# First GEMM by halves, w_in decoded in eight pieces, and zero matmuls ahead of the first scores

## The chip, the cores and the metric

One core of one Trainium2 chip. The metric is the device time of one execution in microseconds (us). Three runs of the kernel before took 536.71, 537.28 and 537.35 us; the median is 537.28.

## What is computed

The reference chains three parts, in float32 at the interface:

```python
attn_out = _attn_ref(q, k, v)              # (2, 8, 576, 64): heads 0-3 see a plain window of 32,
                                           # heads 4-7 a window dilated by 4
x = attn_out.transpose(0, 2, 1, 3).reshape(1152, 512)
h = x @ w_in                               # w_in is 512 x 1024, float64
e = np.exp(h - h.max(-1, keepdims=True))
solu = h * (e / (e.sum(-1, keepdims=True) + 1e-09))
ln = (solu - mu) / np.sqrt(var + 1e-06) * g_ln
x = ln @ w_out                             # w_out is 1024 x 512, float64
p = domain_probs / (domain_probs.sum(-1, keepdims=True) + 1e-09)
for e in range(4):                         # w1: 4 x 512 x 1024, w2: 4 x 1024 x 512
    out += p[:, e:e + 1] * (np.maximum(x @ w1[e], 0.0) @ w2[e])
```

## The kernel before, in words

Every matrix product of full precision is done as three products of float32r halves (high x high, high x low, low x high), so each operand is split into a high and a low part.

The work is cut into generators whose steps (one `yield` each) stand one by one in the text `ORDER` (line 25 on). The scheduler is manual: a loop over `ORDER` (from line 614) runs the next step of the generator named, and each engine executes its own instructions in just that order. Each engine waits for the instruction at the head of its queue; SyncE (SP) issues the loads in the order of the `l..` entries. A "+" behind a name sends the step's variable instruction to another engine: `pick()` then gives GpSimd and not VectorE, and `copy()` VectorE and not ScalarE.

- `UP.t.b`, `UD.t.b` (`att_U`, line 238): an attention unit, of the plain or the dilated heads, third t of sequence b; 12 units of 12 steps. Step 1: mask matmuls (line 245) and scores (line 254) on TensorE; 2: maximum (line 262) and 3: subtraction (line 264) on VectorE; 4: exponential on ScalarE (line 267); 5: sum, 6: reciprocal on VectorE; 7: product into a probability tile `pd` (line 273, `pick`); 8: six transposes (line 279); 9: copy to `pt` (`copy`); 10: product with v (line 292); 11: high part to `xhi` (`copy`); 12: low part to `xlo` (line 231, VectorE).
- `VI.j` (`conv_in`, line 195): w_in row block j, decoded from float64 by `convert` (line 169): two ScalarE steps (lines 173, 175), shift (line 177) and merge (line 179) on VectorE, addition (line 181, `pick`), high part (`copy`), low part (line 206, `pick`). Blocks 1, 2 and 3 are decoded 1024 columns at a time, block 0 in two halves (`VI.0`, `VI.4`). `VO.j.t` (`conv_out`) does the same for w_out in eight pieces of 512 columns; its low part is line 222 on VectorE.
- `H.t` (`moe_H`, line 315): 128 tokens of the first GEMM, 24 matmuls of 512 columns (line 321); the four row blocks of w_in are the outer loop and the two halves of the output columns the inner, and `HCUT` says how many row blocks make a step. Then maximum, exponential, product with sum (line 330) and scaling.
- `T.t` (`moe_T`): transposes of those 128 tokens (line 349), squares (line 351), high and low part. `X.c.dp` (`moe_X`): second GEMM (line 370), 384 tokens, half of the outputs; `XCUT` cuts it into steps, each for one or more of the four w_out blocks.
- `sc` (`scales`, line 580): small VectorE steps and one power on GpSimd for the normalisation. `WP`, `XQ`, `WV`: splits of w1, x and w2 for the expert part (line 402); `u`, `d` (`up`, line 483 in `product`; `down`, line 553): the two products of the experts, which then run in a plain loop to the end.

PSUM has two pools of two tiles: `psa` for scores, transposes and products with v, `psm` for H and X; a step that needs a third tile waits until the tile before the last has been read.

Ahead of `ORDER`, GpSimd builds the mask and VectorE clears the three probability tiles (lines 124, 125):

```python
for pd in pds:
    nc.vector.memset(pd, 0.0)
```

Of the kernel before, what the change touches and what calls it, by code (L numbers as in the profile page):

```python
# [28 lines left out]
UP.1.0 UP.0.0 lI.3 UP.0.0 UP.0.0 UD.2.0 VI.4+ UP.1.0 UP.2.0 lD.1 lO.0.0 lvp.2.0 VI.2 VI.1+ UP.1.0+ UD.1.0 UD.1.0 H.0 UD.1.0 UD.0.0 VI.2 UD.2.0 VI.2
UP.1.0 UD.0.0 VI.2+ UP.0.1 VI.1 VI.1 UP.1.0 UP.0.1 UD.0.0 VI.3 UP.0.1 UD.0.0 UD.0.0 VI.3 H.0 UD.2.0 UP.1.0 UD.2.0 VI.3 VI.3 UP.1.0 UP.2.0 UD.0.1 UP.0.1  # L30
lO.0.1 UP.1.0 UP.2.0 H.1 lP.1.1 VI.3+ UD.1.1 UD.0.1 VI.2 misc H.1 UP.2.0+ VI.3 VI.3+ UP.0.1 VO.0.1 UD.0.1 UD.0.1 VI.2 VO.0.1 UD.2.0 H.0 VO.0.0 H.0
UD.0.1 UD.1.1 UP.0.1 UD.1.1 VO.0.0 UD.2.0 endE UP.2.0 UP.0.1 UD.1.1 UD.2.0 UP.0.1 UD.0.1 H.0 UP.2.0 VO.0.1 VO.0.0 H.1 UP.2.0 H.0 VO.0.0 lvp.0.1 H.1
UP.0.1 lvd.2.1 H.0 UD.0.1+ VO.0.1 UP.2.0 UP.2.0 H.0+ H.1 UP.0.1 VO.0.0+ T.0 lvd.0.1 UP.0.1+ UP.0.1 VO.0.1+ UD.1.1 VO.0.0 T.0 VO.0.0 lO.1.0 T.0 H.2
UD.2.1 lO.1.1 T.0 UD.2.1 VO.1.0 UD.2.1 UD.0.1 H.1 H.1 UD.0.1 UD.2.1 H.2 VO.1.0 UD.2.1 VO.1.0 UD.0.1 H.1+ UD.1.1 T.1 UD.0.1 VO.1.0 UD.1.1+ VO.0.1 VO.1.1
T.1 H.2 H.3 UD.0.1 lvd.1.1 UP.2.1 T.1+ T.1 VO.1.0+ UD.1.1 H.2 VO.1.0 H.3 lO.2.0 UD.2.1 VO.0.1 UD.1.1 UP.2.1 lvp.1.1 H.2 UD.2.1+ VO.1.1 UP.2.1 VO.1.0
VO.2.0 VO.1.1 UD.1.1 VO.1.1 H.2+ H.3 VO.1.1+ VO.2.0 T.2 UD.1.1 T.2 VO.2.0 H.3 VO.2.0 UD.1.1 lO.2.1 UP.2.1 H.3 VO.1.1 H.4 T.2 VO.2.1 VO.1.1 VO.2.1 T.2
VO.2.1 H.3+ UP.2.1 UP.1.1 UP.2.1 UD.2.1 H.4 lvp.2.1 UP.1.1 VO.2.0+ VO.2.0 H.4 VO.2.1 lO.3.0 X.0.1 UP.1.1 UP.1.1 VO.2.1 UD.2.1 H.4 VO.2.0 VO.2.1 UP.2.1+
VO.2.1 VO.3.0 UP.1.1 VO.3.0 UP.2.1 UD.2.1 UP.1.1 UP.2.1 lO.3.1 UP.1.1+ VO.3.0 UD.2.1 VO.3.1 VO.3.0 X.0.0 UP.1.1 VO.3.1 VO.3.1 UD.2.1 VO.3.0 VO.3.0
VO.3.1 VO.3.1 H.4 UP.2.1 VO.3.1 VO.3.0 VO.3.1 X.0.1 UP.2.1 UP.1.1 UP.2.1 UP.1.1 endA UP.1.1+ X.0.1 X.0.0 T.3 X.0.0+ H.5 UP.1.1 T.3 T.4 H.5 T.4 H.5 H.6
H.5 T.3 H.5 H.7 H.5+ H.6 T.4 T.3 H.6 H.6 T.5 T.5 T.4 H.7 H.8 H.6 T.5 H.7 T.6 T.6 H.7 T.5 T.6+ X.1.0 X.1.0 H.8 H.8 T.6 H.7+ H.8 H.8+ T.8 T.7 X.1.1 T.7  # L40
T.8 endH X.1.0 T.7 lW.0 sc X.1.1 T.8 T.7 XQ.0 WP.0 T.8 X.1.1 WP.0+ WP.0 XQ.0 XQ.0 WP.0 WP.0+ XQ.0 X.2.0 WP.0 X.2.1 XQ.0 XQ.0 XQ.0 XQ.0 X.2.0 XQ.0 XQ.0+
WP.0 XQ.0 WP.0 XQ.0 WP.0+ lV.0 XQ.0 XQ.0 WP.0 WP.0 endX WP.0+ XQ.0 XQ.0 u.0 WP.0 WP.0 WP.0+ u.0 WP.0 u.0 WV.0 lW.1 X.2.1+ XQ.1 XQ.1 XQ.1 u.0 u.0 u.0
WV.0 u.0 u.0 WP.0 XQ.1 XQ.1 u.0 u.0 XQ.1 WP.0 XQ.1 u.0 u.0 WV.0 u.0 u.0 XQ.1 u.0 u.0 u.0 XQ.1 XQ.1 u.0 u.0 u.0 u.0 XQ.1 u.0 u.0 u.0 u.1 XQ.1 u.1 XQ.1
XQ.1 u.1 u.1 XQ.1 XQ.1 u.1 WP.1 WV.0 u.1 u.1+ u.1 u.1 WP.1 WP.1 WP.1 u.1 WP.1 u.1 u.1 u.1 u.1 u.1 WP.1 u.1 u.1 d.2 d.1 WP.1+ WP.1 u.1 d.2 lV.1 u.1 u.1
# [672 lines left out]
```

## Time and profile before

| | |
|---|---|
| runs, median (lowest to highest) | 537.28 us (536.71 to 537.35) |
| profiled execution | 536.57 us |
| its span | 534.8 us |
| TensorE busy | 520.2 us (97%), 3660 matmuls |
| VectorE busy | 349.6 us (65%) |
| ScalarE busy | 198.9 us (37%) |
| GpSimd busy | 166.8 us (31%) |
| granted TensorE clock | 1.00 |

The span runs from the first to the last instruction; all times inside it count from its start. "Busy" is the time in which an engine executes an instruction; the rest is waiting. A share over the whole span hides that stages differ: the first 30 us, the attention stage to some 94 us, the two GEMMs to some 155 us and the experts each have their own limit.

### The profile page before, as it was taken

To read this page: it belongs to the slowest core of one execution; us is meant where nothing else is said; L and a number is where in the kernel's file an instruction comes from. 1 tells how busy PE (TensorE), PEld (TensorE's weight loads), DVE (VectorE), ACT (ScalarE), POOL (GpSimd) and SP (SyncE) were. 2 spreads that over 40 slices of the span, in tenths; PEclk is the share of its full clock that TensorE was granted. 3 is DMA by queue.
4 is the path that set the end of the run, shared out by engine and by line. 5 is a ranking of instruction groups with operands and counts; after the bars stand their busy time and mean duration, and the time that the engine had idled before them with its cause. 6 is when DMAs were issued, how large, how long until landed. Compare 5 with 4: busy or idle time off the path is not lost.

```text
span 534.8 us, 8713 instructions
## 1 busy us (share of the span) xinstructions
PE 520.2 (97%) x3660; PEld 465.8 (87%) x3660; DVE 349.6 (65%) x472; ACT 198.9 (37%) x302; POOL 166.8 (31%) x121
## 2 busy tenths in 40 slices
...
GB/s 326 406 214 101 64 135 1 0 1 20 60 132 65 119 2 0 159 1 0 98 60 1 1 157 1 0 102 58 1 1 158 0 1 79 1 1 0 2 80 97
DMA packets 16856, 36.21 MB, mean 68 GB/s; under 512 B 3376, under 2 KB 3632, under 8 KB 16176
## 3 DMA queue, kind: packets, MB, share of 16 engines
...
q8 instruction: 29, 0.48, 0.4%
...
## 4 chain that ended last, share of the span: by engine, by line
PE 94%; DMA 2%; DVE 2%; ACT 1%; issue 0%; SPq 0%; DVEq 0%; ACTq 0%
PE pm L553 18%; PE pa L553 18%; PE pm L483 17%; PE pa L483 17%; PE pm L321 10%; PE pm L370 8%; PE pa L292 2%; PE pa L349 2%; DMA draw<-in_moe_w_in_dram 2%; PE pa L279 1%; DMA rw<-in_moe_w_dram 1%; PE pa L254 1%; ACT pt L159 0%; DVE sm L264 0%; PE pa L245 0%
## 5 line engine op out<-in xcount | busy, mean ns | idle before, releaser
L496 DVE SCALAR_TENSOR_TENSOR hl<-ct,hh 128x512 fp32r<-128x512 f32 (+1 forms) x64 | 61.5, 980 | 32.4 <-ACT hh L494 32.4
L494 ACT ACTIVATE hh<-ct 128x512 fp32r<-128x512 f32 (+1 forms) x64 | 42.2, 682 | 51.9 <-DVE ct L526 22.9
L553 PE MATMUL pm<-wh,hh 128*128 128x512 f32 (+1 forms) x148 | 56.9, 384 | 0.6 <-DVE xf L558 0.6
L483 PE MATMUL pa<-xoh,hl 128*128 128x256 f32 (+1 forms) x192 | 56.9, 296 | 0.0
L483 PE MATMUL pm<-xoh,hl 128*128 128x256 f32 (+1 forms) x192 | 56.8, 296 | 0.0
L483 PE MATMUL pm<-xol,hh 128*128 128x256 f32 (+1 forms) x192 | 56.8, 296 | 0.0
L483 PE MATMUL pa<-xol,hh 128*128 128x256 f32 (+1 forms) x192 | 56.8, 296 | 0.0
L553 PE MATMUL pm<-wl,hh 128*128 128x512 f32 (+1 forms) x148 | 56.8, 384 | 0.0
L483 PE MATMUL pm<-xoh,hh 128*128 128x256 f32 (+1 forms) x192 | 56.8, 296 | 0.0
L483 PE MATMUL pa<-xoh,hh 128*128 128x256 f32 (+1 forms) x192 | 56.8, 296 | 0.0
L553 PE MATMUL pm<-wh,hl 128*128 128x512 f32 (+1 forms) x148 | 56.7, 383 | 0.0
L553 PE MATMUL pa<-wl,hh 128*128 128x512 f32 x144 | 56.1, 390 | 0.0
L553 PE MATMUL pa<-wh,hh 128*128 128x512 f32 x144 | 56.1, 390 | 0.0
L553 PE MATMUL pa<-wh,hl 128*128 128x512 f32 x144 | 56.0, 389 | 0.0
L510 POOL TENSOR_TENSOR ct<-ct,ct 128x512 f32<-128x512 f32 (+1 forms) x15 | 22.4, 1492 | 78.7 <-ACT ct L508 52.6
L402 POOL TENSOR_TENSOR wl<-wl,wh 128x1024 fp32r<-128x1024 f32 x7 | 16.9, 2413 | 95.7 <-ACT wh L159 95.7
L558 DVE SCALAR_TENSOR_TENSOR xf<-pm,pr,xf 128x512 f32<-128x512 f32 (+1 forms) x33 | 24.1, 730 | 32.9 <-PE pm L553 32.9
L159 ACT CAST wh<-wl 128x1024 fp32r<-128x1024 f32 x16 | 16.8, 1053 | 71.0 <-PE pa L553 40.6
L558 DVE SCALAR_TENSOR_TENSOR xf<-pa,pr,xf 128x512 f32<-128x512 f32 x31 | 23.1, 746 | 29.4 <-PE pa L553 29.4
L483 PEld LDWEIGHTS pm<-xoh,hh 128*128 128x128 f32 x192 | 36.4, 190 | 0.3
L483 PEld LDWEIGHTS pm<-xol,hh 128*128 128x128 f32 x192 | 36.4, 190 | 0.3
L483 PEld LDWEIGHTS pa<-xol,hh 128*128 128x128 f32 x192 | 36.4, 190 | 0.3
...
## 6 DMA issues: line engine op xcount, KB each, us to landing
...
```

The source lines that it names most:

```text
L159: nc.scalar.copy(out, in_)
L292: nc.tensor.matmul(po[64 * row:64 * row + 64, 0, o:o + 96], lhsT=vv, rhs=pt[:, j, :, g, :], start=True, stop=True)
L321: nc.tensor.matmul(pm[:, n, :], lhsT=xx[:, kk, cols], rhs=ww["in", kk][:, 512 * n:512 * n + 512], start=(n_ == 0 and i < 2), stop=(n_ == K ...
L349: nc.tensor.transpose(pa[:, f // 4, (f % 4) * 128:(f % 4) * 128 + 128], e[:, f // 4, (f % 4) * 128:(f % 4) * 128 + 128], ident)
L370: nc.tensor.matmul(pm[:, dd, 0:CW], lhsT=w_, rhs=x_[:, f, :], start=(f == 0 and i == 0), stop=(f == KF - 1 and i == 2))
L402: pick().tensor_tensor(out=out, in0=a, in1=b, op=op)
L483: nc.tensor.matmul(ps[:, ff, 0:n], lhsT=a[:, kk, fc], rhs=b[:, kk, :], start=kk == 0 and m == 0, stop=kk == 1 and m == 2)
L494: nc.scalar.activation(out=hv, in_=src, func=AF.Relu)
L496: nc.vector.scalar_tensor_tensor(out=lv, in0=src, scalar=0.0, in1=hv.bitcast(F32), op0=ALU.max, op1=ALU.subtract)
L510: poolv().tensor_tensor(out=c12, in0=c21, in1=c22, op=ALU.add)
L553: nc.tensor.matmul(po[:, u, 0:dn], lhsT=h_[:, f, cols], rhs=w_, start=(f == 0 and i == 0), stop=(f == 3 and i == 2))
L558: nc.vector.scalar_tensor_tensor(out=acc[:, t, dc], in0=po[:, u, 0:dn], scalar=pr[:, t, e:e + 1], in1=acc[:, t, dc], op0=ALU.mult, op1=ALU ...
```

## The change

- `wz`, a tile of zeros, is cleared by VectorE, and `warm(8)` puts eight matmuls of zeros, 512 columns each, first on TensorE; `warm.4` in the order puts four more behind the scores of `UD.2.0`. Their PSUM tile belongs to `psm`; nothing reads it.
- The three probability tiles are cleared on GpSimd.
- w_in is loaded and decoded in eight pieces of 512 columns (`VI.0` to `VI.7`; j + 4 is the second half of block j), each with its own raw tile; the decoded words go through four buffers of 512 columns (`cvp`), which w_out shares, and w_out's raw words through two (`crp`).
- `moe_H` has the halves of the output columns as the outer loop and the row blocks as the inner; a half is finished before the other begins. `HCUT` and `XCUT` cut H and X finer.
- The order is another throughout, up to the expert loop.
- g_ln and the domain probabilities are laid out on the host so that each partition's values lie together in memory.
- `up` reads `hb[s]` inside `block`; that issues nothing.

```diff
-KORD = (0, 1, 2, 3)
-HCUT = (1, 1, 2, 2, 4, 2, 4, 4, 4)
-XCUT = (2, 2, 4)
+HCUT = (1, 1, 1, 1, 2, 2, 2, 4, 4)
+XCUT = (1, 1, 2)
...
+lP.0.0 UP.0.0 UP.0.0 UP.0.0 UP.0.0 UP.0.0 UP.0.0 UP.0.0 UP.0.0 lI.0 VI.0 VI.0 lD.0 UD.1.0 UP.0.0 VI.0 VI.0 UD.0.0 UD.1.0 UD.1.0 UD.1.0 VI.0+
+VI.0 VI.0+ UD.0.0 UD.0.0 UD.1.0 UD.1.0 lvp.0.0 UP.0.0 UP.0.0 UP.0.0 UD.0.0 lP.1.0 UP.1.0 UD.0.0 UD.1.0+ UD.0.0 UP.1.0 UP.1.0 UD.0.0+ lI.7 VI.7 UD.2.0
+VI.7 lI.2 lI.3 UD.2.0 VI.2 warm.4 UD.0.0 VI.2 lvd.0.0 lvp.1.0 UD.2.0 lD.1 lI.1 UP.2.0 UP.1.0 VI.7 VI.7 VI.2 UP.1.0 UP.1.0 UP.1.0+ lvd.1.0
...
+T.1 H.3 UP.1.1 H.4 VO.3.0 VO.2.0+ VO.0.0 VO.2.0 VO.3.0 UP.1.1+ H.4 H.4 H.4 UP.1.1 T.2 UP.1.1 H.3 H.3+ UP.2.1+ UP.2.1 VO.2.0 VO.3.0
+VO.3.0 VO.3.0 VO.3.0 H.4 UP.2.1 X.0.0 X.0.0 VO.3.0 H.4 H.4 lO.2.1 UP.1.1 VO.2.1 UP.2.1 UP.1.1+ UP.1.1 X.0.1 X.0.1 lO.3.1 VO.3.1 VO.3.1 VO.2.1
+VO.2.1 VO.2.1 VO.3.1 VO.2.1 VO.2.1 VO.2.1 X.0.0 H.4+ VO.3.1 VO.3.1 VO.3.1 VO.3.1 X.0.0 endA X.0.0 UP.2.1 UP.2.1 X.0.1 X.0.1 T.3 T.3 X.0.1+
+T.4 T.4 H.6 H.6 H.6 H.6 H.6 H.6 H.6 H.5 H.5 H.5 H.5 H.5 H.7 H.7 T.3 T.3 H.6+ H.5 H.5 H.5
+T.6 T.4 T.4 T.6 T.6 T.5 T.5 T.5+ H.7 T.5 H.7 H.7 H.7+ H.8 H.8 H.8 H.8 H.8 H.8+ X.1.0 X.1.0 X.1.0
+T.6 T.8 T.7 T.7 X.1.0 T.8 sc endH T.8 T.8 X.1.0 lW.0 T.7+ X.1.1 T.7 X.1.1 X.1.1 X.1.1 WP.0 XQ.0 X.1.1+ WP.0+
...
+    wz = const.tile([128, 512], BF16, name="wz")
+    nc.vector.memset(wz.bitcast(U32), 0)
+    wps = psm.tile([128, 2, 512], F32, name="pm", tag="pm")
+
+    def warm(n):
+        for i in range(n):
+            nc.tensor.matmul(wps[:, i % 2, :], lhsT=wz[:, 0:128], rhs=wz, start=True, stop=True)
+
+    warm(8)
...
-    cv = at.enter_context(tc.tile_pool(name="cv", bufs=1))
+    cvp = at.enter_context(tc.tile_pool(name="cvp", bufs=4))
+    crp = at.enter_context(tc.tile_pool(name="crp", bufs=2))
...
     for pd in pds:
-        nc.vector.memset(pd, 0.0)
+        nc.gpsimd.memset(pd, 0.0)
...
     def load_in(j):
         j, half = j % 4, j // 4
-        if half:
-            nc.sync.dma_start(out=dins[j][:, 1024:2048].bitcast(I64), in_=w_in[128 * j:128 * j + 128, 512:1024])
-            return
-        r = dins[j] = erp.tile([128, 2048], I32, name=f"draw{j}", tag=f"draw{j}")
-        n = 512 if j == 0 else 1024
-        nc.sync.dma_start(out=r[:, 0:2 * n].bitcast(I64), in_=w_in[128 * j:128 * j + 128, 0:n])
+        r = dins[j, half] = erp.tile([128, 1024], I32, name=f"draw{j}{half}", tag=f"draw{j}{half}")
+        nc.sync.dma_start(out=r.bitcast(I64), in_=w_in[128 * j:128 * j + 128, 512 * half:512 * half + 512])
...
-        sl = slice(512 * half, 512 * half + (512 if j == 0 else 1024))
+        sl = slice(512 * half, 512 * half + 512)
...
-        a = (erp.tile([128, 1024], F32, name="eva", tag="eva") if j % 2 else cva)[:, sl]
-        yield from convert(dins[j][:, 2 * sl.start:2 * sl.stop], a)
+        a = cvp.tile([128, 512], F32, name="cva", tag="cva")
+        yield from convert(dins[j, half], a)
...
     def moe_H(t):
         pm = psm.tile([128, 2, 512], F32, name="pm", tag="pm")
         cols = slice(128 * t, 128 * t + 128)
-        for n_, kk in enumerate(KORD):
-            seq = [(xhi, whi, n) for n in range(2)] + [(xhi, wlo, n) for n in range(2)] + [(xlo, whi, n) for n in range(2)]
-            for i, (xx, ww, n) in enumerate(seq):
-                nc.tensor.matmul(pm[:, n, :], lhsT=xx[:, kk, cols], rhs=ww["in", kk][:, 512 * n:512 * n + 512],
-                                 start=(n_ == 0 and i < 2), stop=(n_ == KD - 1 and i >= 4))
-            if n_ % HCUT[t] == HCUT[t] - 1:
-                yield
+        for n in range(2):
+            for kk in range(KD):
+                for i, (xx, ww) in enumerate(((xhi, whi), (xhi, wlo), (xlo, whi))):
+                    nc.tensor.matmul(pm[:, n, :], lhsT=xx[:, kk, cols], rhs=ww["in", kk][:, 512 * n:512 * n + 512],
+                                     start=(kk == 0 and i == 0), stop=(kk == KD - 1 and i == 2))
+                if (n * KD + kk) % HCUT[t] == HCUT[t] - 1:
+                    yield
...
     def load_misc():
-        nc.sync.dma_start(out=g_sb, in_=g_ln.rearrange("(f p) -> p f", p=128))
-        nc.sync.dma_start(out=pr_raw, in_=probs.rearrange("(t p) e -> p t e", p=128))
+        nc.sync.dma_start(out=g_sb, in_=g_ln)
+        nc.sync.dma_start(out=pr_raw, in_=probs.rearrange("p (t e) -> p t e", t=NTT))
...
+    d["moe_g_ln"] = d["moe_g_ln"].reshape(-1, 128).T
+    p = d["moe2_domain_probs"]
+    d["moe2_domain_probs"] = p.reshape(-1, 128, p.shape[1]).transpose(1, 0, 2).reshape(128, -1)
```

## Rows read from the trace of the kernel before

**Rows 1.** Windows: length, busy time (instructions) of PE, PEld, DVE, ACT, POOL, PEclk, DMA

```profile
10.00:15.00 5.00, 3.91 (x133) 2.26 (x123) 4.49 (x11) 3.10 (x6) 2.35 (x3) 1.00 1.02 425
...
22.93:85.54 62.61, 61.63 (x702) 50.08 (x701) 57.92 (x96) 50.53 (x79) 23.03 (x16) 1.00 0.39 135
...
138.40:531.00 392.60, 392.02 (x2312) 358.19 (x2313) 248.97 (x298) 114.17 (x174) 129.92 (x80) 1.00 0.14 47
```

**Rows 2.** Timeline of TensorE, first 30 us: start, duration, instruction, count, idle before

```profile
3.49 0.48 PE L245 MATMUL pa<-mask,identb 128*128 128x192 bf16 x2 [3.49 <-POOL mask L114]
5.68 0.97 PE L254 MATMUL pa<-qkP 64*32 64x64 f32 x48 [1.72 <-DMA qkP<-in_qkp_dram]
...
9.16 0.97 PE L254 MATMUL pa<-qkD 64*32 64x64 f32 x48 [2.08 <-DMA qkD<-in_qkd_dram]
...
16.10 1.54 PE L279 MATMUL pa<-ident,pd 128*128 128x128 f32 x6
...
19.04 1.35 PE L279 MATMUL pa<-ident,pd 128*128 128x128 f32 x6
...
23.64 0.82 PE L279 MATMUL pa<-ident,pd 128*128 128x128 f32 x6
```

**Rows 3.** Timeline of VectorE, first 45 us

```profile
3.68 2.87 DVE L125 MEMSET pd<- 128x960 f32 x3
6.47 0.36 DVE L177 TENSOR_SCALAR cva<-cva 128x512 uint32<-128x512 uint32 x1
...
10.17 0.56 DVE L262 TENSOR_REDUCE st<-pa 128x6 f32<-128x384 f32 x1 [1.56 <-PE pa L254]
...
14.31 0.68 DVE L177 TENSOR_SCALAR cva<-cva 128x512 uint32<-128x512 uint32 x1
...
43.15 1.22 DVE L330 SCALAR_TENSOR_TENSOR e<-e,pm 128x1024 f32<-128x1024 f32 x1
```

**Rows 4.** VectorE's groups, 0 to 95 us: count, busy, mean ns, idle before

```profile
L179 DVE SCALAR_TENSOR_TENSOR eva<-draw,eva 128x1024 uint32<-128x1024 uint32 x2 | 2.4, 1220 | 0.0
...
L181 DVE CUSTOM_DVE_ANT_0 cva<-cvr,cva 128x1024 uint16<-128x1024 uint16 x3 | 2.1, 686 | 0.0
...
L179 DVE SCALAR_TENSOR_TENSOR cva<-draw,cva 128x512 uint32<-128x512 uint32 x2 | 1.4, 684 | 0.0
```

**Rows 5.** Timeline of ScalarE, first 36 us

```profile
4.41 0.67 ACT L173 ACTIVATE draw<-draw 128x512 int32<-128x512 uint32 x1 [2.39 <-DMA draw<-in_moe_w_in_dram]
...
13.40 0.53 ACT L267 ACTIVATE sm<-sm 128x384 f32<-128x384 f32 x1 [0.40 <-DVE sm L264]
```

**Rows 6.** Timeline of GpSimd, first 36 us

```profile
0.73 0.20 POOL masks.py:197 MEMSET ident<- 128x128 f32 x1 [0.29 <-POOLq L700]
...
4.69 0.12 POOL L121 MEMSET mhalf<- 128x9 f32 x1
...
13.88 1.79 POOL L273 TENSOR_TENSOR pd<-sm,st 128x384 f32<-128x384 f32 x2
```

**Rows 7.** Timeline of SyncE's DMA queue

```profile
23.22 6.26 SPq L605 DMA_DIRECT2D pr_raw<-in_moe_domain_probs_dram  x1
31.35 2.31 SPq L142 DMA_DIRECT2D vp<-in_vpw_dram  x1
```

**Rows 8.** The chain that ended last: start, duration, what

```profile
84.19 4.36 PE pm L370 x24
...
89.37 4.38 PE pm L370 x24
93.75 0.87 PE pa L349 x8
...
525.13 2.72 PE pa L553 x12
```

**Rows 9.** Timeline of VectorE, end of the attention stage

```profile
84.13 1.41 DVE L222 SCALAR_TENSOR_TENSOR wl<-cva,g_sb,wh 128x512 fp32r<-128x512 f32 x2
```

**Rows 10.** TensorE's waits: who waited for whom, total, times, longest

```profile
PE pm L370 <- DVE hl L231: 0.7, 1, 0.7
```

**Rows 11.** Timeline of VectorE around T.7, T.8 and X.2

```profile
131.51 0.17 DVE L584 SCALAR_TENSOR_TENSOR esq<-esq,nmx 128x9 f32<-128x9 f32 x1 [7.07 <-ACT e L351]
...
134.41 1.22 DVE L231 TENSOR_TENSOR hl<-pa,hh 128x1024 fp32r<-128x1024 f32 x1
...
137.12 1.22 DVE L231 TENSOR_TENSOR hl<-pa,hh 128x1024 fp32r<-128x1024 f32 x1
```

More of the change, by code (lines that the diff above doesn't have):

```diff
@@ L29 @@
[L29 to L44, printed above, removed]
@@ new lines @@
+VI.7+ UD.0.0 lI.5 VI.3 VI.3 UP.2.0 UD.0.0 UP.2.0 VI.2 UD.0.0 UD.0.0 UD.2.0 UD.2.0 UD.2.0 UP.2.0 VI.3 UP.2.0 H.0 UP.2.0 UP.1.0 UP.1.0 UD.1.0
+UD.1.0 VI.3 UD.0.1 UD.0.1 VI.1 UD.2.0+ UD.0.1 VI.1 VI.1 VI.2+ UP.1.0 lP.0.1 lvd.2.0 UP.1.0 VI.2 UD.1.1 UP.1.0 UD.1.1 UP.2.0+ UD.1.1 VI.1 VI.1
+VI.3+ UD.2.0 UP.0.1 UP.0.1 lI.6 UP.0.1 lI.4 UD.2.0 misc UD.2.0 VI.7 VI.3 VI.7+ H.1 lP.1.1 UD.1.0 VI.1 VI.1 H.0 UD.2.0 UD.2.0 UD.0.1
+UD.0.1 H.1 UD.1.0 UD.1.0 VI.4 UD.0.1 UD.0.1 VI.4 VI.3+ VI.4 UP.2.0 VI.4 UP.2.0 UD.2.1 UD.2.1 UD.2.1 lvd.2.1 UP.0.1 UP.0.1 VI.2+ UP.0.1 UP.0.1
@@ new lines @@
+VI.4+ VI.5 VI.5 VI.5 H.1 VI.5 UD.1.1 H.0 UD.0.1 VI.4 UD.1.1 UD.1.1 UD.0.1 lvp.2.0 UP.2.0 UP.2.0 lvp.0.1 H.0 VI.5+ UP.2.0 VI.4 VI.6
+VI.6 lO.1.1 lvd.0.1 UD.1.1 UP.0.1 lvp.1.1 UP.0.1 VI.6 VI.6 VI.5 VI.5 H.1 UD.2.1 UD.2.1 UD.2.1 UD.0.1 UD.0.1 UD.0.1 UP.1.1 VI.6+ VO.1.1 UP.1.1
+VO.1.1 UP.1.1 VO.1.1 VI.6 VI.6 VO.1.1 H.1 H.0 H.0 UD.1.1 UD.1.1 UP.2.1 H.0 UP.2.1 UP.2.1 UP.2.1 H.0 H.0 UD.2.1+ lO.1.0 VO.1.0 UD.2.1
+VO.1.0 H.0 UP.0.1 VO.1.1+ H.1 VO.1.0 H.1 H.1 UP.0.1+ UP.0.1 H.0 UD.2.1 UD.2.1 UD.2.1+ UP.1.1 VO.1.0 UD.2.1 lvd.1.1 UD.1.1 H.0+ UP.2.1 H.2
@@ new lines @@
+H.2 H.2 endE T.0 H.1 lO.0.1 VO.0.1 VO.0.1 VO.1.0+ H.2 VO.0.1 VO.1.0 VO.1.1 VO.1.1 VO.0.1 H.1 H.1 T.0 VO.0.1+ lO.0.0 H.2 H.2
+H.2 H.2 UD.1.1 UD.1.1 VO.0.0 lO.2.0 T.0 UP.2.1 H.2 VO.0.0 T.0 H.2 H.3 H.3 H.1+ VO.0.0 VO.0.0 H.3 H.3 H.3 lvp.2.1 VO.0.0+
+H.3 H.3 H.3 VO.2.0 VO.0.0 VO.2.0 VO.0.1 H.2 H.2 VO.1.0 T.1 T.1 T.1 H.3 VO.0.1 VO.2.0 VO.2.0 T.2 lO.3.0 T.2 T.2 UP.1.1
+T.1 H.3 UP.1.1 H.4 VO.3.0 VO.2.0+ VO.0.0 VO.2.0 VO.3.0 UP.1.1+ H.4 H.4 H.4 UP.1.1 T.2 UP.1.1 H.3 H.3+ UP.2.1+ UP.2.1 VO.2.0 VO.3.0
+VO.3.0 VO.3.0 VO.3.0 H.4 UP.2.1 X.0.0 X.0.0 VO.3.0 H.4 H.4 lO.2.1 UP.1.1 VO.2.1 UP.2.1 UP.1.1+ UP.1.1 X.0.1 X.0.1 lO.3.1 VO.3.1 VO.3.1 VO.2.1
```

24 lines of the change are left out of this document (13 added, 11 removed).

## The prediction

> **What bounds the kernel now.** First the windows [rows 1]: from 138.4 us to 531.0 us TensorE is busy 392.02 of 392.60 us, so nothing is to be had there unless a new wait appears. In the attention stage (22.93 to 85.54) TensorE is busy 61.63 of 62.61 us, but VectorE 57.92: two engines are full. From 10 to 15 us VectorE is busy 4.49 of 5 and TensorE 3.91. TensorE's timeline [rows 2] shows the start: its first matmul at 3.49, scores only at 5.68 after a wait of 1.72 for the q/k load, the next unit at 9.16 after 2.08. VectorE's timeline [rows 3] shows its side: three memsets of probability tiles (2.87 us), the first w_in shift at 6.47, then 1.56 of waiting until the second unit's maximum at 10.17; after that the gaps are few. The chain [rows 8] shows the end of the stage: TensorE passes from X.0 (from 84.19, and 89.37) to T.3 at 93.75 without a hole, while VectorE ends its last w_out piece at 85.54 [rows 9], only some 7 us of X.0 work ahead. One late hole is left: X.2 waits 0.7 us [rows 10] for a low part that VectorE wrote at 137.12 [rows 11].
>
> So the time is TensorE's work plus what it loses up to T.3, plus that hole. TensorE's own matmuls are the same after the change, but for 12 zero matmuls.
>
> **The start.** VectorE clears wz, then TensorE runs 8 zero matmuls of 512 columns. No row has their price: at the 2.72 us for 12 of 512 columns that the last stage pays [rows 8] it is 1.8 us for 8; at the mask pair's 0.48 us for 2 x 192 columns [rows 2] it is 5.1. I take 3.4, the middle, since the mask pair has a fixed part. They start near 1 us, so scores come at 4.9 instead of 5.68; between the bounds 4.4 (the load, now first on SP; the first load of before had landed at 4.41 [rows 5]) and 6.6. Then all eight steps of unit P.0 stand first, each waiting for the one ahead: scores to 5.9 (0.97), maximum and subtraction 1.1, exp 0.52 [rows 5], sum, reciprocal and product 1.45, so transposes start at 9.0 and take 1.35 [rows 2] to 10.4. The dilated scores behind them on TensorE end at 11.3: the second unit's maximum comes at 11.35 instead of 10.17, with the first unit's five vector steps done instead of two. Taking 2.87 us of memsets off VectorE buys nothing here, since VectorE then waits for this chain.
>
> The memsets on GpSimd: a 128x128 one takes 0.20 us [rows 6], so 128x960 takes between 0.86 (VectorE's row) and 1.53. They follow the memset of mhalf, which ends at 4.81; the first tile is free at 5.7 to 6.3, before the product at 8.3. Cost nothing; if that cover goes, some 0.5 us of the first chain.
>
> **VectorE's queue.** I counted the steps of each order up to the last piece of w_out: 116 before, 128 after, nine of the twelve from w_in. A wide step (128x1024) takes 1.22 us, a half one 0.68 [rows 4]: three wide pieces become six, +0.14 per pair of steps, so +0.8 for shifts and merges, and one addition goes from GpSimd to VectorE (+0.69): +1.5. By the + marks the rest differs by two more products, one copy to xhi, one unit's last two steps that now come earlier, less one copy of pt and one of hh: +0.9. Sum: VectorE has 2.4 us more to do up to that piece, and between that piece and T.3 TensorE has 6.3 us (X.0.0's last quarter 2.09, half of X.0.1 4.18) against 7.1 before. If VectorE's waits stayed as they were, T.3 would move 1 to 2 us back.
>
> They don't stay, so I walked the new queues by hand, each step at the duration of its row, behind its inputs and its PSUM buffer (two each). By 22.1 the third unit's xlo is written: level with before. At 41.2 the low part of w_in piece 5 is done, where VectorE's queue adds up to 31.7 us; before, the sum of 32.1 (H.0's product) is reached at 44.37 [rows 3]. This gain of some 3 us comes from H by halves: pieces of H need only half a row block of w_in, and the four small buffers let ScalarE run ahead. The zero matmuls in mid-queue (warm.4, 1 to 2 us) delay P.2's scores, VectorE waits 0.45 for them. Loads stay ahead: in bytes at the rate of the first 30 us every load lands before its step; the tightest is vp for P.2, 31 against 35.6. It stands behind the probabilities' load, whose issue held SP 6.26 us before [rows 7]; the new layout makes it one run per partition, and I take that as gone; if not, P.2 comes 1 to 2 us late.
>
> At the end of the stage the walk gives the gain back: the last two w_out pieces are decoded late, one behind the other through ScalarE and VectorE. H.4's exponential makes VectorE wait 1.4, X.0.0's third quarter starts at 84.0 after a hole of 1 us, its last at 86.6, T.3 at 92.9. The walk has no slowing by sharing: before, the stretch from 22.93 takes 62.6, its steps add up to 55.1 and its gaps to 4.7, 2.8 stay unexplained. A third of that falls on TensorE's path (0.9; the rest in stretches where another engine is last): T.3 at 93.8 against 93.75. **The stage comes out level**, between -3 and +2.
>
> One rule of the Trainium skill speaks against the moves to GpSimd. The rows: the same 128x512 shift takes 0.36 at 6.47 and 0.68 at 14.31 [rows 3], where GpSimd runs products from 13.88 [rows 6]. GPSIMD Engine Reference, Specifications, says that GpSimd shares its SBUF interfaces with VectorE, to the harm of VectorE's two-port modes. The trace agrees. In the late stage, where the new order gives GpSimd about twenty additions of w1 and x, nine casts on VectorE would pay 0.32 each, 2.9 us, and twenty additions of 0.68 leave it: no loss on the path.
>
> **The late hole.** In the new order three quarters of X.1.0 come ahead of T.8 and T.7, so that 10.4 us of X lie behind T.7 instead of 8.4. T.7 and T.8's squares, the scales with GpSimd's power (131.51 to 134.41 [rows 11]), T.8's low part and T.7's copy and low part end 9.1 us behind T.7. The hole of 0.7 goes, with 0.2 of the stream's restart: -0.9. Next late would be u.0 (first product 27 us behind T.7, its inputs by 23). The end of the kernel and the expert loops don't change.
>
> **Sum:** 0.1 - 0.9 = -0.8 on the profiled execution (536.57, span 534.8); the median of the runs, 537.28, lies 0.7 above it, so about 536.5. The chance of this is 0.42, its own range 535.4 to 537.7.
>
> **Rivals.** (a) The gain of 3 us at 41 us survives, since w_out pieces don't wait: ScalarE's spacing is shorter than its mean durations. For it: before, VectorE lost only 4.7 to gaps; against: both last loads need a buffer to come free. T.3 at 91.0: 533.6 us; chance 0.18.
> (b) The zero matmuls make TensorE fast from the start. The rows: six transposes take 1.35 at 19.04 and 0.82 at 23.64 [rows 2], though the granted clock reads 1.00 (2.4 GHz) all along [rows 1]; ahead of the change TensorE had run with gaps under 0.2 us from 16.1. Then transposes and two blocks of scores of the first chain shrink by 1.0 in all, and VectorE starts so much sooner: 535.5; chance 0.12. TensorE: Matmul & The Clock Gate (Part 1) states that the array starts throttled and that activity releases it; by that rule this rival is the case. Against: TensorE stands idle 3 us right behind P.0's scores.
> (c) Slower: the last w_out pieces decide. All of the 2.8 us falls on the path, because X.0.0's third quarter follows VO.2.1 and its last VO.3.1; it decides from a VectorE finish later than 87.5 us. T.3 at 95.8, +2.1, less 0.9: 538.5, and 539.6 if the load of the last piece also waits a full microsecond for its buffer; chance 0.24.
> (d) It doesn't do what it says: the scales or T.7 come late again and the hole stays: 537.4; chance 0.04.
>
> **Numbers.** Differences under 0.2% (1.07 us) can't be told from none here. Of the forecast's 0.42, 0.16 lies below 536.2 and 0.26 within; (a) and most of (b) are faster, (d) same, (c) slower but for a little: faster 0.44, same 0.32, slower 0.24. Range 533.4 to 539.6.
>
> **What would show it.** Scores of P.0 near 4.9, the second unit's maximum near 11.3; VectorE at H.0's end 2 to 3 us ahead; TensorE's holes between X.0.0's quarters, released by VectorE or ScalarE's wl/wh; T.3 near 93.8; X.2 without a wait. I am wrong if TensorE is starved elsewhere (u.0, or H behind w_in pieces 1 and 6), if GpSimd's additions are late, or if T.3 comes before 91 or behind 96.

## The result, and the profile after

The change makes the kernel slower: 541.76 us median (541.46 to 541.92) against 537.06 in the same session, ratio 1.0087 (1.0070 to 1.0105). The forecast was 536.5, its range ended at 539.6.

The profiled execution took 541.88 us with a span of 540.1. At the end of its last matmul it is 5.17 us behind the one before (536.72 against 531.55). Three marks split that. By TensorE's timeline T.3 starts at 97.97 instead of 93.59 (its piece of the chain [rows 8] starts at 93.75), 4.38 later; from there to u.0's first product it takes 61.04 us instead of 61.39, 0.35 less; from u.0 to the end 1.14 more. So nearly all of it is lost up to T.3.

Windows of the kernel after, from 5 to 25 us and the late ones (columns: window, length, busy us of TensorE, its weight loads, VectorE, ScalarE, GpSimd, then granted clock, DMA share and GB/s):

```profile
5.00:10.00 5.00, 1.66 (x53) 1.44 (x53) 3.15 (x7) 1.62 (x3) 2.32 (x3) 0.92 0.98 399
10.00:15.00 5.00, 4.64 (x155) 3.33 (x155) 3.10 (x7) 2.52 (x5) 1.90 (x2) 0.74 0.99 374
15.00:20.00 5.00, 3.01 (x102) 2.08 (x79) 3.29 (x9) 2.90 (x6) 2.24 (x3) 1.00 1.02 413
20.00:25.00 5.00, 3.21 (x74) 2.32 (x73) 3.63 (x9) 2.77 (x5) 2.61 (x2) 1.00 1.04 400
...
85.00:98.00 13.00, 12.83 (x73) 12.43 (x74) 6.98 (x15) 5.06 (x8) 0.00 (x0) 1.00 0.00 1
98.00:140.00 42.00, 42.00 (x232) 38.11 (x231) 21.61 (x28) 20.12 (x29) 4.21 (x2) 1.00 0.07 26
140.00:160.00 20.00, 19.59 (x116) 19.27 (x115) 19.13 (x24) 3.60 (x6) 9.19 (x6) 1.00 0.07 24
160.00:185.00 25.00, 24.16 (x173) 23.41 (x172) 19.86 (x24) 11.64 (x17) 15.68 (x10) 1.00 0.43 149
```

From 10 to 15 us VectorE was busy 4.49 before [rows 1] and is busy 3.10 now; up to 25 us both engines stand idle for long stretches. Late, TensorE loses 0.41 us from 140 to 160 and 0.84 from 160 to 185. TensorE's timeline of the start [rows 2], and VectorE's three long waits beside it [rows 3]:

```profile
1.19 3.59 PE L84 MATMUL pm<-wz 128*128 128x512 bf16 x8 [1.19 <-DVE wz L79]
...
5.03 0.92 PE L267 MATMUL pa<-qkP 64*32 64x64 f32 x48
9.29 1.54 PE L292 MATMUL pa<-ident,pd 128*128 128x128 f32 x6 [3.34 <-DVE pd L286]
...
11.09 0.97 PE L267 MATMUL pa<-qkD 64*32 64x64 f32 x48
...
14.73 0.66 PE L267 MATMUL pa<-qkP 64*32 64x64 f32 x41
17.38 0.31 PE L267 MATMUL pa<-qkP 64*32 64x64 f32 x7 [1.99 <-issue]
...
21.14 0.71 PE L305 MATMUL pa<-pt,vd 128*64 128x96 f32 x10
23.57 0.55 PE L305 MATMUL pa<-pt,vd 128*64 128x96 f32 x6 [1.73 <-issue]
...
97.97 0.71 PE L362 MATMUL pa<-ident,e 128*128 128x128 f32 x5
```

```profile
12.09 0.56 DVE L275 TENSOR_REDUCE st<-pa 128x6 f32<-128x384 f32 x1 [1.79 <-PE pa L267]
...
17.75 0.56 DVE L275 TENSOR_REDUCE st<-pa 128x6 f32<-128x384 f32 x1 [1.53 <-PE pa L267]
...
25.05 0.87 DVE L244 TENSOR_TENSOR xlo<-pa,xhi 128x384 fp32r<-128x384 f32 x1 [1.32 <-ACT xhi L175]
```

TensorE waits 3.34 us for P.0's probabilities; the scores of D.1 stand behind the transposes, though their load had landed at 8.45. Then it stops twice, 1.99 and 1.73 us, in the middle of a block and without waiting for any engine. VectorE's waits follow from these three.

The first stop lies behind matmul 223 of the stream (8 + 2 + 48 + 6 + 2 + 48 + 2 + 48 + 16 + 2 + 41). In the kernel before a stop of 1.01 us ends at 15.50, also behind 223 (nine groups of 2 or 48, and 21). The second lies 127 further on. Both follow a packet on the instruction queue, seen here in the DMA view of 14.8 to 15.8 us: so TensorE's instructions come in blocks, and a stop is the wait for the next.

```profile
q8 instruction: 1, 0.02, 6.0%
```

### The profile page after: what moved, and what is told of

It reads as the page before. It is cut to its first block, busy times and chain, and to the rows that moved or that the text cites. A ratio compares the mean times of both kernels' runs of the same rounds, so it can differ in the third digit from the quotient of the medians.

```text
span 540.1 us, 8775 instructions
## 1 busy us (share of the span) xinstructions
PE 523.3 (97%) x3672; PEld 467.0 (86%) x3672; DVE 347.8 (64%) x464; ACT 197.4 (37%) x308; POOL 198.6 (37%) x145
## 4 chain that ended last, share of the span: by engine, by line
PE 76%; DVE 7%; ACT 2%; issue 2%; POOL 2%; DMA 1%; ACTq 0%; POOLq 0%; SPq 0%; DVEq 0%
PE pm L566 18%; PE pa L566 18%; PE pm L496 16%; PE pa L496 16%; PE pm L334 4%; PE pm L383 2%; PE pa L362 1%; DVE hl L244 1%; DVE wl L235 1%; DMA cvr<-in_moe_w_out_dram 1%; ACT e L364 1%; POOL xol L415 1%; DVE cva L193 1%; ACT wh L233 0%; DVE sw L415 0%
## 5 line engine op out<-in xcount | busy, mean ns | idle before, releaser
L509 DVE SCALAR_TENSOR_TENSOR hl<-ct,hh 128x512 fp32r<-128x512 f32 (+1 forms) x64 | 62.9, 1003 | 36.1 <-ACT hh L507 36.1
L415 POOL TENSOR_TENSOR hl<-sw,hh 128x512 fp32r<-128x512 f32 x20 | 30.0, 1501 | 27.8 <-ACT hh L175 24.7
L523 POOL TENSOR_TENSOR ct<-ct,ct 128x640 f32<-128x640 f32 (+1 forms) x15 | 22.1, 1474 | 45.9 <-ACT ct L521 40.8
L496 PEld LDWEIGHTS pa<-xoh,hh 128*128 128x128 f32 x192 | 36.4, 190 | 0.4
```

What stands on the lines that cost most here:

```text
L415: pick().tensor_tensor(out=out, in0=a, in1=b, op=op)
L496: nc.tensor.matmul(ps[:, ff, 0:n], lhsT=a[:, kk, fc], rhs=b[:, kk, :], start=kk == 0 and m == 0, stop=kk == 1 and m == 2)
L509: nc.vector.scalar_tensor_tensor(out=lv, in0=src, scalar=0.0, in1=hv.bitcast(F32), op0=ALU.max, op1=ALU.subtract)
L523: poolv().tensor_tensor(out=c12, in0=c21, in1=c22, op=ALU.add)
```

## Experiments

Two theories of the start were on the table: F, that the stops cost it, and P, that the wait for P.0's chain does; beside them Q or V (VectorE's longer queue), S and S' (whatever is won at the start is lost again) and W (the GEMM by halves). The expectations count the matmul ahead of the stop from nought, as 222. Runs were timed in turns with the kernel before; its medians were 536.88 to 537.25.

**Small parts alone, in the kernel before.** Eight zero matmuls first:

```diff
+    nc.vector.memset(wz.bitcast(U32), 0)
...
+    warm(8)
```

> The kernel before with only the clearing of wz and the eight zero matmuls added ahead of everything. Theory F: the stop of 1.01 us behind matmul 222 stands eight matmuls earlier in the work, at the 13th instead of the 21st score of its block; VectorE had other work there and did not wait, so the time stays within 0.5 us of 537.1. Rival K (the zero matmuls lift TensorE's clock for good): the transposes at 16.10 and 19.04 fall from 1.54 and 1.35 to 0.82 us, some 1.2 us in all, 536.0. Rival Z (the zero matmuls hold up the first scores): scores at 6.3 instead of 5.68, 537.7.

536.75, ratio 0.9995 (0.9986 to 1.0003). The stop again follows matmul 223, eight earlier in the work, and the transposes at 15.78 and 18.68 still take 1.54 us. Memsets and layout:

```diff
-        nc.vector.memset(pd, 0.0)
+        nc.gpsimd.memset(pd, 0.0)
...
+        nc.sync.dma_start(out=g_sb, in_=g_ln)
...
```

> The kernel before with two small parts of the change alone: the three memsets of the probability tiles on GpSimd and the new layout of the scales and probabilities. Theory: VectorE is free 2.87 us earlier at 3.6, but has nothing to do before the first load and the second unit's maximum (10.17, behind its load); the issue of 6.26 us on SP goes, which nobody waited for; same within 0.4 us, 537.0. Rival: VectorE's queue of the whole stage shifts forward by what its early decode steps gain, up to 0.7: 536.3. Rival on the other side: GpSimd's memsets come late for the first product or hold up its first decode step: 537.6.

537.09, ratio 1.0003 (0.9994 to 1.0013). Neither part moves the time.

**The stops.** The changed kernel without zero matmuls:

```diff
-    warm(8)
...
-... VI.2 warm.4 UD.0.0 ...
+... VI.2 UD.0.0 ...
```

> The changed kernel without its 12 zero matmuls, all else as it is. Theory F (instructions in blocks): TensorE's two stops without a wait (1.99 us behind its 222nd matmul, 1.73 us behind its 349th) belong to the count of matmuls, not to the work. Then the first stop stands again behind matmul 222, which is now 8 matmuls further in the work, behind the last scores of P.1 instead of inside them, and the second behind D.0's last product with V; VectorE's waits of 1.53 us (17.75) and 1.32 us (25.05) shrink to under 0.5 us each. With 0.6 us from an earlier start of the scores T.3 comes at 94.5 to 95 instead of 97.97, and the time is 538.3 (537.5 to 539). Rival Q (VectorE's longer queue, 2.9 us more of work, sets the stage whatever TensorE does at the start): only the 0.6 us of the start are won, the stops stay inside P.1's scores and D.0's products, T.3 at 97.3, 541.2. Rival K (the zero matmuls keep the clock up): the early transposes get slower than 0.82 us and the time is the same or above 541.8.

540.80 (540.17 to 541.76), ratio 1.0070 (1.0057 to 1.0082). The place is as F has it: the stop (1.37 us) follows matmul 223, now behind P.1's scores, the next is 0.98 us, and VectorE starts D.0's low part at 22.39 instead of 25.05. But T.3 comes at 97.74. The windows of this run, and a line of TensorE's timeline, show where the 2.7 us go:

```profile
28.00:30.00 2.00, 0.58 (x16) 0.32 (x5) 1.86 (x4) 0.00 (x0) 0.87 (x1) 0.93 0.98 375
30.00:32.00 2.00, 2.00 (x53) 1.64 (x54) 0.73 (x2) 0.78 (x2) 0.00 (x0) 0.50 1.04 396
32.00:34.00 2.00, 2.00 (x42) 1.67 (x28) 1.51 (x3) 1.96 (x5) 1.32 (x2) 0.72 0.41 153
...
29.90 1.23 PE L283 MATMUL pa<-ident,pd 128*128 128x128 f32 x5 [1.27 <-issue]
```

A third stop (1.27 us, to 29.90) and, right behind it, the granted clock at 0.50 (1.2 GHz) while TensorE is full.

Two loads held back:

```diff
+            nc.gpsimd.memset(r.bitcast(F32)[:, 0:1], 0.0)
...
+            nc.gpsimd.memset(qkD[1][:, 0:1], 0.0)
```

> The changed kernel with two loads held back by a GpSimd memset of one column of their tiles: w_in piece 2 (and what SP has behind it) until GpSimd has done piece 0's addition (11.7 us), the q/k load of the second batch until D.0's product (17.2 us). Theory F: each block of TensorE's instructions (16,384 bytes on the instruction queue) takes 3.2 to 3.8 us to start because load packets stand ahead of it; with the load queue short at 11.7 and 17.4 us the two packets start up to 3 us sooner, the stops of 1.99 and 1.73 us fall under 0.5 us each, VectorE's waits of 1.53 and 1.32 us with them: D.0's low part at 22.5 instead of 25.05. The time by that 539.2, or 540.5 if a later block and the loads pushed back by some 2 us take half of it back, as in the run without zero matmuls. Rival (the 6.2 us per block are the instruction queue's own, whatever else runs): stops as long as before and the loads later, 542.5.

540.46 (539.79 to 541.67), ratio 1.0059 (1.0046 to 1.0072). The first packet now runs between 12.0 and 13.4 us, the second between 18 and 19 instead of 21.2 to 22.3, and both stops are gone: D.0's low part starts at 22.16. So it is the loads ahead of them that hold the blocks up. But a third stop, of 1.41 us, ends at 28.87, the clock falls to 0.50 behind it, and T.3 stands at 97.65.

```profile
28.87 0.33 PE L277 MATMUL pa<-qkD 64*32 64x64 f32 x10 [1.41 <-issue]
...
32.00:34.00 2.00, 2.00 (x18) 1.68 (x17) 1.97 (x3) 1.07 (x2) 2.00 (x2) 0.50 1.02 386
```

VectorE's steps moved into its waits (piece 7's are shown; piece 3's are moved likewise):

```diff
-... UP.1.0 UP.1.0 UD.0.0+ lI.7 VI.7 UD.2.0 VI.7 ...
+... lI.7 VI.7 VI.7 VI.7 VI.7 UP.1.0 UP.1.0 UD.0.0+ UD.2.0 ...
```

> The changed kernel with four steps of VectorE moved forward in the order: the shift and the merge of w_in piece 7 ahead of P.1's maximum, and those of piece 3 ahead of D.0's low part; their inputs are there (ScalarE ends piece 7's at 16.28, piece 3's at 22.2). They fill 1.1 us each of the two waits of VectorE that TensorE's stops cause (1.53 at 17.75, 1.32 at 25.05). Theory V (VectorE's queue carries what it loses at the start to the end of the attention stage): VectorE stands 2 us earlier from 27 us on, T.3 at 96 instead of 97.97, 539.7. Rival S (the supply of TensorE's instructions, some 127 matmuls in 6.2 to 6.8 us as long as loads run, sets the pace up to 31 us): the scores, transposes and products come when they came, VectorE waits for them instead, and the time is within 0.5 us of 541.8.

541.39, ratio 1.0086 (1.0074 to 1.0098): S. VectorE gets ahead, then waits for TensorE 1.00 us at 28.36.

**P.0's chain.** The changed kernel with D.1's scores ahead of P.0's transposes:

```diff
-... UP.0.0 UP.0.0 lI.0 VI.0 VI.0 lD.0 UD.1.0 UP.0.0 VI.0 ...
+... UP.0.0 lI.0 VI.0 VI.0 lD.0 UD.1.0 UP.0.0 UP.0.0 VI.0 ...
```

> The changed kernel with the scores of the second unit (D.1) put ahead of P.0's transposes on TensorE; nothing else. TensorE waited 3.3 us for P.0's probabilities (5.95 to 9.29) with those scores behind it, whose load had landed at 8.45; VectorE waited 1.79 us for them (12.09). Theory P (P.0's eight steps first cost the start): the second unit's maximum comes at 10.3, the count of matmuls runs 1.5 us ahead, the block behind matmul 222 is asked for that much sooner, and the whole start moves 1.5 to 1.8 us forward: T.3 at 96.3, 540.2. Rival S' (what is won at the start is lost again at 28 to 34 us, by a later block of instructions or by the clock, as in the runs without zero matmuls and with gates): T.3 at 97.7, 541.4.

539.49 (539.12 to 540.92), ratio 1.0050 (1.0037 to 1.0062): 2.3 us of the 4.7 with one matmul group moved. TensorE's timeline of this run, VectorE's line for D.0's low part, and the window in which the two runs above have the low clock:

```profile
8.51 0.72 PE L267 MATMUL pa<-qkD 64*32 64x64 f32 x48 [2.08 <-DMA qkD<-in_qkd_dram]
9.38 0.85 PE L292 MATMUL pa<-ident,pd 128*128 128x128 f32 x6
...
20.95 0.55 PE L305 MATMUL pa<-pt,vd 128*64 128x96 f32 x7 [0.97 <-issue]
...
95.07 0.71 PE L362 MATMUL pa<-ident,e 128*128 128x128 f32 x5
...
22.43 0.87 DVE L244 TENSOR_TENSOR xlo<-pa,xhi 128x384 fp32r<-128x384 f32 x1 [0.79 <-ACT xhi L175]
...
32.00:34.00 2.00, 2.00 (x22) 1.65 (x18) 1.68 (x5) 1.42 (x5) 2.00 (x2) 1.00 0.45 167
```

Behind P.0's scores TensorE now waits for D.1's load alone. The first stop is gone, the second is down to 0.97, and D.0's low part starts at 22.43, as early as without zero matmuls (22.39) or with loads held back (22.16). Unlike their gains this one lasts: there is no third stop, the clock reads 1.00 from 17 us on, and T.3 is 2.90 us earlier in this profile, which is of the fastest run (539.12). The same part put alone into the kernel before:

```diff
-VI.0 UD.0.0 VI.0 UP.0.0 UP.0.0 UD.0.0 ...
+VI.0 VI.0 UP.0.0 UP.0.0 UP.0.0 UP.0.0 UP.0.0 UP.0.0 UP.0.0 UD.0.0 UD.0.0 ...
```

> The kernel before with one part of the change: P.0's steps two to eight (maximum to transposes) put one behind the other at the start, ahead of the second unit's scores on TensorE, P.0's product on VectorE instead of GpSimd. Theory P: the second unit's scores, there from 9.1 us, wait for P.0's transposes (probabilities near 10.5, transposes to 12); TensorE's lost time at 35 us rises from 16.9 to 18.5 or more, T.3 by 1.6 to 2.9: 538.7 to 540, 539.3. Rival: P.0's early end gives H.0 and later steps their inputs sooner and the start evens out: 537.1.

542.87, ratio 1.0106 (1.0092 to 1.0119): 5.9 us, more than expected.

```profile
10.64 1.54 PE L281 MATMUL pa<-ident,pd 128*128 128x128 f32 x6 [3.92 <-DVE pd L275]
...
14.74 0.48 PE L247 MATMUL pa<-mask,identb 128*128 128x192 bf16 x2 [1.34 <-DVE sm L266]
...
17.36 0.50 PE L247 MATMUL pa<-mask,identb 128*128 128x192 bf16 x2 [1.25 <-DVE sm L266]
```

The direction is P's. The size is not the part's alone: behind the late scores every unit waits 1.3 us for VectorE to free a PSUM buffer, since the rest of the old order was laid out for scores in advance.

**The pieces and the halves, in the kernel before.** w_in in eight pieces:

```diff
-lI.1 ... VI.1
+lI.1 lI.5 ... VI.1 VI.5
```

> The kernel before, in its own order, with one part of the change: w_in loaded and decoded in eight pieces of 512 columns (each wide step becomes two steps one behind the other), w_out's buffers as in the changed kernel, H as before. This prices the part of VectorE's longer queue that comes with the pieces: 0.8 us by the rows for shifts and merges, 1.5 with the low parts. Theory V: VectorE's last w_out piece comes 1 to 1.5 us later than 85.54; T.3 by up to that: 537.0 to 538.4, 537.8. Rival: the pieces let ScalarE and TensorE start earlier and win back what VectorE pays: 537.0.

539.65 (538.54 to 540.69), ratio 1.0048 (1.0033 to 1.0063): V in direction, but 2.6 us where 0.8 was expected. Its runs lie in two groups, three from 538.5 to 539.0 and three from 540.3 to 540.7. The profile is of one at 538.55: VectorE ends the last w_out piece 1.11 us later than [rows 9] and T.3 starts 1.24 later; what the other group loses no profile shows. The GEMM by halves:

```diff
-        for n_, kk in enumerate(KORD):
+        for n in range(2):
+            for kk in range(KD):
...
```

> The kernel before with one part of the change: the first GEMM by halves of its output columns. H.0 and H.1 take their steps where they stood, but each of the first four has three matmuls (0.68 us) instead of six, and the other twelve follow the fourth; the other row blocks have the same steps. Theory W (TensorE has too little long work while loads run): at 22.15 and 27.85 TensorE has 0.7 us less to do, waits the sooner for VectorE, and is 0.7 to 1.4 us behind at T.3: 537.8 to 538.5, 538.1. Rival: the scores and transposes behind those matmuls come 0.7 us sooner, VectorE gains by it, and the time is the same, 537.0.

541.32 (540.99 to 542.26), ratio 1.0082 (1.0068 to 1.0096): W, but 4.1 us where 1.1 was expected. H's matmuls in windows, of the kernel before, of this run and of the changed kernel (columns: window, length, TensorE's busy us and matmuls, weight loads):

```profile
0.00:30.00 30.00, 3.42 (x12) 2.02 (x12) 1.00 0.95 371
30.00:40.00 10.00, 6.14 (x23) 4.03 (x24) 1.00 0.55 152
```

```profile
0.00:30.00 30.00, 2.46 (x6) 0.97 (x6) 1.00 0.96 375
30.00:40.00 10.00, 3.81 (x12) 2.01 (x13) 1.00 0.57 140
```

```profile
0.00:30.00 30.00, 0.97 (x3) 0.48 (x3) 0.94 0.96 366
30.00:40.00 10.00, 4.10 (x15) 2.58 (x15) 1.00 0.32 116
```

By 40 us 35 matmuls of H are done before, 18 in either of the others: the 17 that are missing are 3.9 us at 0.227 each, and TensorE idles where they stood. In this run T.3 starts 4.46 us later. In the order before, then, halves cost more than whole rows; the changed order was made for them, so the 4.1 us can't be taken as a share of its 4.7.

**The late stage.** Two tries to take away u.0's wait:

```diff
-... XQ.1 XQ.1 XQ.1 XQ.1+ XQ.1 XQ.1+ u.0 u.0 u.0 u.0 ...
+... XQ.1 u.0 u.0 XQ.1 u.0 u.0 u.0 u.0 XQ.1 XQ.1+ XQ.1 XQ.1+ ...
```

> The changed kernel with the casts of the second part of x (XQ.1, its last four steps) put behind the first two ScalarE copies of u.0 in the order, nothing else. Theory: u.0's first copy waited 4.7 us on ScalarE's queue (160.44 to 165.13) behind two casts that wait for a subtraction on GpSimd and one on VectorE; with it first the copy comes at 161.5, TensorE's wait of 0.8 us in u.0 goes with its slow surroundings of 0.3: 540.6. Rival: XQ.1 is then late for u.1, which waits as long: 541.8.

541.70, ratio 1.0086 (1.0073 to 1.0100).

```diff
-... XQ.1 XQ.1 XQ.1 XQ.1 XQ.1+ XQ.1 XQ.1+ u.0 u.0 u.0 u.0 ...
+... u.0 u.0 u.0 u.0 XQ.1 XQ.1 XQ.1 u.0 u.0 XQ.1 XQ.1+ XQ.1 XQ.1+ ...
```

> The changed kernel with the first four steps of u.0 (two products, ScalarE's copy, VectorE's addition) ahead of XQ.1's second to fourth in the order, and the next two ahead of its fifth. The run with the copy alone moved left TensorE's wait at 0.9 us, now for VectorE's addition, which stood behind XQ.1's subtraction (waiting for GpSimd until 161.9) and a low part of 1.48. Theory: with both ahead the wait in u.0 goes, 0.8 to 1.1 us less: 540.8. Rival: XQ.1 then comes late for u.1 and TensorE waits there as long: 541.7.

541.88, ratio 1.0088 (1.0074 to 1.0102). The rival both times: the wait at 165 us goes, and one of 0.9 comes at 178.0, for u.1's addition on VectorE, behind w2's low part. (The second expectation takes that wait for one in u.0; in both runs it is u.1's.) A third, together with the start of the run at 539.5:

```diff
-... u.1 u.1 WV.0 WV.0 u.1 u.1 XQ.1
+... u.1 u.1 u.1 u.1 WV.0 WV.0 XQ.1
...
-... T.7+ X.1.1 T.7 X.1.1 ...
+... T.7+ X.1.1 T.7 sc X.1.1 ...
```

> The changed kernel with D.1's scores ahead of P.0's transposes (as in the run at 539.5), and three moves in the late stage: u.0's first two additions and copies ahead of the second part of x (as tried before), the low part of w2's first half behind u.1's first addition on VectorE (it made TensorE wait 0.89 us at 178.0 once u.0's own wait was gone), and the scales' last two operations behind T.7's low part. Theory: with both waits of the u stage gone 1.1 us, with X.2's wait of 0.4 us gone 0.4 more: 538.1. Rival: the late stage has a third thing that comes as late (w2's low part for the first products of d, or x's second part for u.1), and the time stays at 539.4.

540.47 (539.32 to 540.94), ratio 1.0058 (1.0046 to 1.0071). X.2's wait is gone, but u.1 waits a third time as long, for a low part of x:

```profile
PE pm L496 <- DVE xol L415: 0.9, 1, 0.9
```

And T.3 comes at 96.61, with the very same order up to there as in the run with 95.07: the granted clock reads 0.50 from 10 us to 19.8 here and to 17.0 there (from means of 0.54 and 0.75 in windows of 2 us), and D.0's low part starts at 24.04. So what the start wins is not the same in every execution. With D.0's scores ahead as well:

```diff
-... lD.0 UD.1.0 UP.0.0 UP.0.0 VI.0 VI.0 UD.0.0 UD.1.0 ...
+... lD.0 UD.1.0 UD.0.0 UP.0.0 UP.0.0 VI.0 VI.0 UD.1.0 ...
```

> As the run with start and late moves, and D.0's scores too ahead of P.0's transposes. TensorE waited 0.89 us behind those transposes for ScalarE's copy (10.23 to 11.11), and VectorE 1.17 us for D.0's maximum (12.53). Theory: D.0's scores come at 9.4, its maximum at 11.4, another 0.5 to 1.0 us at the start; 537.4, level with the kernel before. Rival S': the block behind matmul 222 or the transposes, now later by 1.3 us, take it back: 538.1.

540.21 (540.18 to 541.84), ratio 1.0068 (1.0054 to 1.0081): not told apart from the run before it; T.3 at 96.33.

**The late hole of the kernel before.**

```diff
+        yield
...
-... T.7 lW.0 sc X.1.1 T.8 T.7 XQ.0 WP.0 ...
+... T.7 lW.0 sc X.1.1 T.8 T.7 sc XQ.0 WP.0 ...
```

> The kernel before with the scales in two steps: the part up to GpSimd's power where it stood, the two VectorE operations that wait for the power moved behind the low parts of T.8 and T.7. Theory: VectorE no longer waits from 131.7 to 134.4 for the power, the low part that X.2 waits for is written near 135.5 instead of 138.3, and the hole of 0.7 us ahead of X.2 goes: 536.1 to 536.3. Rival: the hole belongs to ScalarE's copies for T.8 and T.7, not to VectorE's wait: 536.9.

536.99, ratio 1.0000 (0.9992 to 1.0008): the hole stays. In this run VectorE's first step on w1 waits 1.37 us for its load (to 136.62), and T.8's low part stands behind it. That step moved too:

```diff
-... sc XQ.0 WP.0 T.8 X.1.1 ...
+... sc XQ.0 T.8 WP.0 X.1.1 ...
```

> The kernel before with the scales in two steps, as in the run before, and VectorE's first step on w1, which waits for its load (landing at 136.5), put behind T.8's low part instead of ahead of it. In the run with the scales alone the low part came at 137.23, right behind that step. Theory: the low part is written by 136.6, X.2 starts without its wait of 0.7 us: 536.2. Rival: X.2's next steps or u.0 wait for w1's later operands instead: 537.0.

535.98 (535.24 to 536.52), ratio 0.9977 (0.9968 to 0.9986). VectorE's timeline and the windows of this run:

```profile
135.56 1.22 DVE L231 TENSOR_TENSOR hl<-pa,hh 128x1024 fp32r<-128x1024 f32 x1
137.89 0.69 DVE L402 TENSOR_TENSOR sw<-rw,rw 128x512 f32<-128x512 f32 x1 [1.11 <-DMA rw<-in_moe_w_dram]
```

```profile
98.00:140.00 42.00, 42.00 (x232) 38.56 (x230) 22.27 (x32) 20.69 (x29) 1.83 (x1) 1.00 0.08 26
```

The low part comes 1.6 us earlier [rows 11], TensorE has no hole. This version beats both kernels, by cutting the scales in two and moving one step.

## Why the prediction was wrong

**The start.** Its first numbers held: P.0's scores at 5.03 (4.9), transposes at 9.29 (9.0). The zero matmuls took 3.59 us; the 3.4 was the middle of its two bounds, 1.8 and 5.1, so that it came so close is in part luck. Alone they cost nothing, nor did the memsets.

The step that failed is "By 22.1 the third unit's xlo is written: level with before". That low part, D.0's, starts at 25.05 and is written at 25.9. The walk let TensorE start each group as soon as its inputs and buffer were there. It named the 3 us of idling behind P.0's scores, but only as an argument on the clock, and gave them no price; and it had no term for stops, though the kernel before has one of 1.01 us. But everything TensorE had to issue stood behind that wait, D.1's scores first, and while loads run, its blocks of instructions come only some 6.2 us apart (stops ending at 17.38 and 23.57).

How much of the 4.7 us belongs to the wait, and how much to the stops, the runs don't separate. Three changes each bring D.0's low part forward by 2.6 to 2.9 us: D.1's scores first, no zero matmuls, and loads held back. The last two run into a third stop and the low clock between 28 and 36 us and end only 1.0 and 1.3 us faster than the changed kernel. D.1's scores first meets neither and ends 2.3 us faster, but it also loses the first stop; the two later runs with the same start are 1.3 and 1.6 faster, late moves included. So between 1.3 and 2.3 us of the loss are the start's.

**The gain of 3 us at 41 us.** It failed altogether. Piece 5's low part ends at 46.79 instead of 41.2. Against the same sum of VectorE's work in the kernel before (44.37) that is 2.4 us behind instead of 3 ahead. Most of the 5.6 us is the start's lag: 3.8 of them are there at D.0's low part. From that part on VectorE took 20.9 us where the walk had 19.1, and 20.6 with D.1's scores first (23.3 to 43.9). The step behind the gain was that "pieces of H need only half a row block of w_in"; it left out that each step of H gives TensorE half the matmuls, and that a row block needs its last piece as before. The run with halves alone shows the sign, in the old order; that this makes up the other 1.8 us is argued.

**VectorE's queue.** The sum of +2.4 was the right kind of term: up to the last w_out piece VectorE is busy 76.08 us, against 76.05 before, which has the memsets' 2.6 in it. What the term is worth in the new order no run shows. In the old one the eight pieces cost 2.6 us in the median, and 1.24 at T.3 in a profile of one of the faster runs, where the prediction's own +1.5 for w_in stood.

**Rival (b), a fast TensorE.** It had no part in it. P.0's transposes still took 1.54 us, and the granted clock fell to 0.50 (1.2 GHz) behind the idle 3.34, as the argument against it said. TensorE's scores do get fast earlier, 48 of them in 0.72 us from 17.89 on where the kernel before takes 0.97 until 18.14. But the zero matmuls don't do that: without them the changed kernel has 0.72 at 14.11, and with them the kernel before has 0.97 at 17.78.

**The last w_out pieces.** Rival (c) had this place: VectorE's finish is 92.94, past its 87.5, the last load waits for its buffer (SP issues it when VectorE's addition at line 195 is done), and the chain of waits runs through both:

```profile
80.35 0.70 DVE cva L195
81.05 0.02 SPq L222
...
81.11 3.43 DMA cvr<-in_moe_w_out_dram
...
92.18 0.76 DVE wl L235
...
92.98 5.15 PE pm L383 x28
```

But TensorE is busy 12.83 of 13 us there, so this is where the lateness shows, not where it arises; and T.3 is 2.2 us behind the rival's 95.8. (The rival's 538.5 and one microsecond make 539.5, not 539.6.)

**Behind T.3.** The hole of 0.7 shrank to 0.41, and the stretch won 0.35 instead of 0.9: VectorE's scales met GpSimd (below). u.0 had its inputs in time, as forecast, and lost 0.84 us for an output, which the walk didn't follow: the first product's copy stands on ScalarE behind two casts that wait for XQ.1's subtractions, the first of them on GpSimd.

```profile
163.87 1.35 ACT L175 CAST xoh<-sw 128x640 fp32r<-128x640 f32 x2 [2.34 <-DVE sw L415]
165.13 0.58 ACT L513 COPY ct<-pa 128x512 f32<-128x512 f32 x1
...
165.76 0.39 PE L496 MATMUL pa<-xoh,w7h 128*128 128x256 f32 x1 [0.84 <-ACT ct L513]
```

**What stays open.** With D.1's scores first the changed kernel is still 2.2 us behind the kernel before, and 3.3 to 3.5 us in the two later runs with that start. The u stage's 1.1 was moved three times and not removed. The rest may be the eight pieces, but their price (1.24 at T.3, 2.6 in the median) was measured in the other order, so the split is argued.
